# An attention and expert kernel on one core: the first token list's tables move to GpSimd, its planner keys are set anew, and eleven weight quarters instead of twelve go out ahead of it

## The chip, the core and the metric

The kernel runs on one core of a Trainium2 chip. Its engines are TensorE (PE, matmuls into PSUM), VectorE (DVE), ScalarE (ACT), GpSimd (POOL) and SyncE (SP). Each runs its own instructions in order, and they wait for each other through semaphores. Sixteen DMA engines serve the queues that SP, ACT and POOL issue to. POOL's own queue converts weights from fp32 to fp16 on the way.

The metric is device microseconds of one launch. Lower is better.

## The reference, cut to what matters

```python
def _attn_ref(q, k, v, is_retrieval, n_sink, window):     # 4 batches, 8 heads, 768 positions, 64 wide
    scores = scale * np.matmul(q, k.transpose(0, 1, 3, 2))
    stream_keep = causal & (is_sink | in_win)             # 4 sinks and a window of 64
    mask = np.where(retr, causal, stream_keep)            # heads 0, 2 and 6 see all that is causal
    a = np.exp(scores - max); a = a / (sum + 1e-09)
    return np.matmul(a, v)

def _moe_ref(x, w_skip, w_gate, w1, w2):                  # x: 3072 tokens x 512; 8 experts, 512 -> 1024 -> 512
    do_compute = x @ w_skip > 0
    out = x.copy(); xc = x[do_compute]
    logits = xc @ w_gate; e_idx = argmax(logits); gate_w = softmax(logits)[e_idx]
    for e in range(E):
        h = np.maximum(xc[e_idx == e] @ w1[e], 0.0)
        y[e_idx == e] = gate_w * (h @ w2[e])
    out[do_compute] = xc + y
```

The attention's output, its eight heads side by side, is x. About half of the tokens skip the experts, and each of the others goes to one expert.

## The kernel before

**Attention.** Two heads of a batch make a pair: 16 pairs, four to a batch, numbered 0 to 15. SP loads q and k of a pair and v of a whole batch. For pair i the steps are named as in the planner's calls:

- `Cq`, `Ck`, `Cv` (L712, L718): cast to fp16, nearly all on GpSimd. `Tq`, `Tk`, `Tv` (L740, L751): transposes on TensorE. `Oq` (ScalarE), `Ok` (VectorE, a few on ScalarE), `Ov` (VectorE): copies out of PSUM.
- `Vw`, `Ow`: the gate's columns v x w_gate are put beside v, so that the weighing gives the gate's logits too. `Kx`, `Vx` (L787, L823): GpSimd's copies for the heads with a window.
- `E`, `X`: scores in chunks of 1024 columns (TensorE, L886 and L898) and their exponential (ScalarE, L908).
- `PV` (L950): the weighing on TensorE, into one PSUM tile `opsa` that has a single buffer, so PV(i) waits for the normalisation of pair i-1.
- `Nr`, `Nl`, `Nx` (L969, L976, L986): reciprocal of the sums, gate logits, and x, on VectorE. Pair 15's Nx is on ScalarE (L1009), in 12 pieces. `Gs` (L1000): the logits of a batch summed over its heads.
- `xo` (L995): a batch's x is stored to the output. "Store 2" and "store 3" below are those of batches 2 and 3; store 3 is issued in two halves, one by SP and one by ACT.

**The two lists.** Tokens are sorted by expert into lists of 128 slots. The first list covers batches 0 to 2 (18 columns of 128 tokens), the second batch 3. `route` and `steps` (L1061, L1232) build them. The first list's chain is: the expert of each token (`mx` to `oh`, VectorE), its rank among the tokens of that expert (`ranks`, TensorE), the slot number in parts (`rsel` to `olo`, VectorE, some on GpSimd), and then two kinds of table: `L` (six of 3 columns, L1202) and `R` (three of 6 columns, L1192). The `slots` matmuls (L1226) multiply L by R; `fin_a` (L1438) turns the result into the indices `idx`.

**Experts.** A gather (L1310) fetches the 128 rows of a slot from the stored output, so the first one needs the indices and the stores of batches 0 to 2. Then come a cast (`cx`), a transpose (`tx`, L1368) and its copy (`ox`), the first matmuls (`F`, L1400), ReLU (ScalarE, L1411), the second matmuls (`Y`, L1422), the addition to the row (`A`, L1428), and a scatter back (L1320).

**Weights.** Each expert has w1 and w2, and each of these is loaded by two DMAs of 1 MB in HBM (512 KB as fp16 in SBUF, L445): a quarter of an expert. All go through GpSimd's queue. `PARTS` (L425) names, for each quarter issued during the attention, the step that it waits for; `late` (L1473) holds the others, issued between gathers and scatters in the order `GORDER`. The very last half matrix goes in two pieces of half that size.

**The order.** Two planners (class `Plan`, L55) write the program, one for the attention and one for the experts. Each step has an engine, an estimated duration, the steps that it needs, and a key. The planner simulates: when an engine is free, the ready step with the lowest key is next. The order in which steps start becomes the order of each engine's instructions. A pair's keys are ten times its number plus a constant of `K` (L647); the first list's steps on VectorE have keys from `K["r"]` up, its tables on GpSimd `K["rp"]`.

## Time and profile before

| | |
|---|---|
| time, median of 3 runs | 188.08 us (187.72 to 188.84) |
| the profiled execution | 187.94 us, of which its span is 186.2 us |
| mean granted TensorE clock | 0.927 |
| busy, share of the span | PE 80%, PEld 65%, DVE 59%, ACT 55%, POOL 70% |
| DMA | 47.12 MB in 27632 packets, mean 253 GB/s |
| HBM | 56.64 MB read, 10.49 MB written |

The profile page has the whole span in 40 slices of 4.65 us; a digit is the busy share in tenths. The attention fills the first half. From slice 21 the engines except GpSimd and the DMA engines have less to do for about four slices: this is where the lists are finished and the first tokens are gathered. After that the experts run to the end. A row of the table of stretches reads: the stretch, its length, the busy time of PE, PEld, DVE, ACT and POOL with the count of instructions, the granted TensorE clock, the mean busy share of the 16 DMA engines, and GB/s. A row of a timeline reads: start, time, engine, line, operation, tiles, shapes, count, and in brackets the idle time before it with what ended it.

### The profile page before, as it was taken

The numbers are of one execution on the slowest core, as the hardware profiler recorded it, in microseconds if no ns is written. First come the engines' busy times: TensorE is split into PE (matmuls) and PEld (weight loads), VectorE is DVE, ScalarE is ACT, GpSimd is POOL, SyncE is SP. The second block draws the span as 40 slices with busy tenths as digits, with TensorE's granted clock in tenths as the row PEclk, the third lists the DMA queues.
The fourth block names the chain that finished last, engine by engine and source line by source line (L and its number), as shares of the span: only waits on it lengthen the run. The fifth ranks groups of instructions, "written<-read, shape, count | busy, mean of one in ns | idle before, by whom it ended". The sixth has DMA issues, their size and how long they took to land.

```text
span 186.2 us, 4856 instructions
## 1 busy us (share of the span) xinstructions
PE 149.0 (80%) x1917; PEld 121.0 (65%) x1929; DVE 108.9 (59%) x245; ACT 103.3 (55%) x145; POOL 131.1 (70%) x229
## 2 busy tenths in 40 slices
PE   0697799699999989989825108999999999979900
PEld 0576688598888778878615108878769787838400
DVE  6565568677878758888994825045444266630320
ACT  2575889599898999999622981322224403403000
POOL 7566888989999999999790556484557788544440
PEclk9999999999999999999995555899999999999975
DMA  5999979998999899999999999999999999999520
GB/s 158 331 321 297 351 235 382 395 327 254 295 398 271 266 306 339 215 226 250 250 253 232 283 318 212 214 260 222 266 210 228 214 232 218 225 223 215 155 78 2
DMA packets 27632, 47.12 MB, mean 253 GB/s; under 512 B 5186, under 2 KB 19138, under 8 KB 27602
## 3 DMA queue, kind: packets, MB, share of 16 engines
q0 software_dynamic: 7312, 21.55, 53.9%
q1 hardware_dynamic: 18560, 23.99, 39.2%
q10 hardware_dynamic: 1730, 1.20, 2.0%
q8 instruction: 17, 0.28, 0.6%
q14 instruction: 13, 0.11, 0.2%
HBM read 56.64 MB, written 10.49 MB: 361 GB/s over the span
## 4 chain that ended last, share of the span: by engine, by line
DMA 41%; PE 23%; issue 11%; POOL 10%; ACT 5%; SPq 3%; DVE 3%; POOLq 0%; ACTq 0%
DMA w<-in_moe_w_dram 14%; DMA out_dram<-x 12%; PE pst L898 9%; DMA xg<-out_dram,idx 6%; PE opsa L950 5%; PE pst L886 4%; DMA out_dram<-xga,idx 4%; POOL out_dram L1320 4%; PE tps L740 4%; SPq L660 3%; DMA kf<-in_k_dram 3%; ACT at L908 3%; POOL w L445 2%; DMA qf<-in_q_dram 2%; POOL xg L1310 2%
## 5 line engine op out<-in xcount | busy, mean ns | idle before, releaser
L908 ACT ACTIVATE at<-pst 128x1024 f16<-128x1024 f32 (+1 forms) x60 | 58.8, 1013 | 9.3 <-PE pst L898 8.7
L1411 ACT ACTIVATE ht<-hps 128x512 f16<-128x512 f32 x32 | 17.1, 600 | 44.4 <-PE hps L1400 44.3
L898 PE MATMUL pst<-qT,k 128*128 128x128 f16 (+2 forms) x308 | 36.3, 238 | 0.7 <-ACT at L908 0.7
L1400 PEld LDWEIGHTS <-w 128*128 128x128 f16 x352 | 32.5, 148 | 3.8 <-DMA w<-in_moe_w_dram 1.5
L1400 PE MATMUL hps<-xT,w 128*128 128x128 f16 (+1 forms) x352 | 33.6, 258 | 1.6 <-DMA w<-in_moe_w_dram 1.0
L780 DVE COPY k<-tps 64x768 f16<-64x768 f16 x27 | 25.8, 954 | 13.1 <-PE tps L740 12.1
L898 PEld LDWEIGHTS <-k 128*128 128x128 f16 x308 | 24.8, 99 | 10.1 <-issue 3.3
L1422 PE MATMUL yps<-w,ht 128*128 128x512 f16 x128 | 30.5, 379 | 0.0
L950 PE MATMUL opsa<-va,at 128*128 128x74 f16 x392 | 21.0, 201 | 0.0
L445 POOL DMA_DIRECT2D w<-in_moe_w_dram x33 | 18.7, 574 | 2.1 <-DMA w<-in_moe_w_dram 1.7
L1422 PEld LDWEIGHTS <-ht 128*128 128x128 f16 x128 | 12.0, 98 | 11.7 <-issue 0.5
L950 PEld LDWEIGHTS <-at 128*128 128x128 f16 x472 | 19.2, 100 | 0.1
L1320 POOL DMA_INDIRECT out_dram<-xg,idx x10 | 10.4, 1037 | 11.8 <-DVE xg L1428 4.1
L886 PE MATMUL pst<-smask,identb 128*128 128x512 bf16 (+3 forms) x52 | 17.3, 345 | 1.6 <-ACT at L908 1.6
L1310 POOL DMA_INDIRECT xg<-out_dram,idx x10 | 11.8, 1179 | 7.8 <-DMA xga<-out_dram,idx 2.1
L986 DVE TENSOR_TENSOR x<-opsa,recs 128x768 f32<-128x768 f32 x15 | 14.1, 943 | 0.0
L1310 POOL DMA_INDIRECT xga<-out_dram,idx x6 | 6.5, 1078 | 10.8 <-DVE idx L1444 6.3
L1428 DVE SCALAR_TENSOR_TENSOR xg<-yps,gsl,xg 128x512 f32<-128x512 f32 x10 | 7.4, 746 | 11.2 <-PE yps L1422 11.0
L718 POOL CAST va<-vf 128x768 f16<-128x768 f32 x16 | 13.1, 823 | 1.1 <-DMA vf<-in_v_dram 0.5
L740 PE MATMUL tps<-ident,q 128*128 128x128 f16 x96 | 8.6, 230 | 6.5 <-DVE q L712 5.9
L712 POOL CAST k<-kf 128x768 f16<-128x768 f32 x15 | 12.4, 825 | 1.7 <-DMA kf<-in_k_dram 1.4
L766 ACT COPY qT<-tps 128x768 f16<-128x768 f16 x16 | 12.8, 800 | 1.0 <-PE tps L740 0.9
(147 smaller groups left out, 252.6 us busy)
## 6 DMA issues: line engine op xcount, KB each, us to landing
w<-in_moe_w_dram POOLq DMA_DIRECT2D x31, 512.0 KB
qf<-in_q_dram SPq DMA_DIRECT2D x16, 384.0 KB, 7.2
kf<-in_k_dram SPq DMA_DIRECT2D x15, 384.0 KB, 6.8
out_dram<-x SPq DMA_DIRECT2D x3, 1536.0 KB, 18.3
out_dram<-x SPq DMA_DIRECT2D x1, 768.0 KB
out_dram<-x ACTq DMA_DIRECT2D x1, 768.0 KB, 8.4
w<-in_moe_w_dram POOLq DMA_DIRECT2D x2, 256.0 KB
kf<-in_k_dram ACTq DMA_DIRECT2D x1, 384.0 KB, 4.4
```

Source lines behind the costliest of these rows:

```text
L445: nc.gpsimd.dma_start(out=wts[e, half][:, c], in_=(w1r, w2r)[half][e][:, c])
L740: nc.tensor.matmul(t[:, n], c16[w, i][:, n].rearrange("p h d -> p (h d)"), C.ident, is_transpose=True, start=(n == 0), stop=(n == NQB - 1))
L780: nc.vector.tensor_copy(to, ti)
L886: nc.tensor.matmul(pst[:, c0 - c * CH:c0 - c * CH + m].rearrange("p (n c) -> p n c", c=P), identb, mv, start=(n == 0), stop=(n == last))
L898: nc.tensor.matmul(pst[:, c0 - c * CH:c0 - c * CH + m * P], lt, qTs[i][:, qb * P:(qb + m) * P], start=(n == 0), stop=(n == last))
L908: nc.scalar.activation(ats[i][:, c * CH:c * CH + cn], psts[i, c][:, :cn], ACT.Exp, scale=SCALE)
L950: nc.tensor.matmul(opss[i][:, hi, qb * VA:(qb + 1) * VA], ats[i][:, b0 + c:b0 + c + P], vb, start=(n == 0), stop=(n == len(todo) - 1))
L1310: moved(nc.gpsimd.indirect_dma_start(out=row(t), out_offset=None, in_=out[:n, :], in_offset=bass.IndirectOffsetOnAxis(ap=idx[:, t:t + 1], ...
L1320: moved(nc.gpsimd.indirect_dma_start(out=out[:n, :], out_offset=bass.IndirectOffsetOnAxis(ap=idx[:, t:t + 1], axis=0), in_=row(t), in_offs ...
L1400: nc.tensor.matmul(hpss[n, b][:, fi, :], w1[:, s, m * b + fi], xTs[n][:, s, :w], start=(fi == 0 and s == 0), stop=(fi == m - 1 and s == DS ...
L1411: nc.scalar.activation(hts[n][:, m * b:m * (b + 1), :w], hpss[n, b], ACT.Relu)
L1422: nc.tensor.matmul(ypss[t], hts[n][:, j, c:c + P], w2[:, j], start=(j == 0), stop=(j == FS - 1))
```

## The change

Three things change in the code.

1. `PARTS` has 11 entries, not 12. Counted from zero, quarters 0 to 5 wait for the same steps as before, quarters 6 to 8 for Cv(15) instead of Vx(13), quarter 9 for Vx(14) instead of Vx(13), and quarter 10 for Vx(14) as before. The twelfth (the second part of expert 2's w2) goes to the late ones and becomes their first. Quarters 6 to 10 have their key lowered by 25.
2. All six L tables of the first list are made on GpSimd, where two (columns 12 to 17) were on VectorE. Two of the three R tables stay on VectorE, but their key is 900, behind every other step there. The planner's estimates for the R tables rise.
3. All constants of `K` are new but `sl`, `Wc` and `xa`.

```diff
-    PARTS = [("Cv", 8), ("Cv", 10)] + [("Vx", 10)] * 4 + [("Vx", 13)] * 4 + [("Vx", 14)] * 2
+    PARTS = [("Cv", 8), ("Cv", 10)] + [("Vx", 10)] * 4 + [("Cv", 15)] * 3 + [("Vx", 14)] * 2
...
-    TAB_DVE = dict(L=(12, 15), R=(6, 12))
+    TAB_DVE = (6, 12)
...
-        K = dict(r=152.5, rp=181, Cq=-144, Ck=-238, Cv=-205, W=-562.5, Tq=-7.5,
-                 Tk=-7.5, Oq=528.5, Ok=-84, OkA=-583, Kx=-828.5, Tv=-2.5,
-                 Ov=-4, Vw=-53, Ow=-472.5, Vx=-124, E=2.5, X=-65, PV=17,
-                 Nr=-46, Nl=114.1, Nx=-227.3, Gs=73.65, sl=-166.5, z=-127,
-                 Wc=-90, xa=-254, rk=-88)
+        K = dict(r=102.5, rp=333, Cq=-109.5, Ck=-161.5, Cv=-228.5, W=-850,
+                 Tq=-8, Tk=-5.5, Oq=421.5, Ok=-309.5, OkA=-680.5, Kx=-1173.5,
+                 Tv=-3.5, Ov=-33.5, Vw=-1, Ow=-941, Vx=-78, E=6, X=70.5,
+                 PV=16.5, Nr=-33.5, Nl=187.1, Nx=23.2, Gs=168.15, sl=-166.5,
+                 z=-19, Wc=-90, xa=-254, rk=-207)
...
-                10 * after[1] + K["W" if after[0] == "Vx" else "Wc"], rate=400)
+                10 * after[1] + K["W" if after[0] == "Vx" else "Wc"] - 25 * (n > 5), rate=400)
...
-                e = v if ph or m in TAB_DVE["R"] else nc.gpsimd
+                e = v if ph or m in TAB_DVE else nc.gpsimd
...
-                        e3 = v if m3 in TAB_DVE["L"] else nc.gpsimd
-                        fns["L", m3] = lambda m=m3, e=e3: e.tensor_tensor(
+                        fns["L", m3] = lambda m=m3: nc.gpsimd.tensor_tensor(
...
-                dve = ph or m in TAB_DVE["L"]
-                op(("r", ph, "L", m), "DVE" if dve else "POOL",
-                   0.9 if ph else 0.55 if dve else 0.8, f["L", m],
-                   [("r", ph, "rl" if ph else "ohi")], k0 + 0.3 if dve else K["rp"])
+                op(("r", ph, "L", m), "DVE" if ph else "POOL",
+                   0.9 if ph else 0.8, f["L", m],
+                   [("r", ph, "rl" if ph else "ohi")],
+                   k0 + 0.3 if ph else K["rp"])
...
-                dve = ph or m in TAB_DVE["R"]
+                dve = ph or m in TAB_DVE
                 op(("r", ph, "R", m), "DVE" if dve else "POOL",
-                   0.6 if ph else 0.55 if dve else 0.9, f["R", m],
+                   0.6 if ph else 0.85 if dve else 1.0, f["R", m],
                    [("r", ph, "oht"), ("r", ph, "glo")],
-                   k0 + 0.25 if dve else K["rp"])
+                   k0 + 0.25 if ph else 900 if dve else K["rp"])
```

## The prediction, made before the changed kernel had run

> **What bounds the kernel now.** I read the page first (clock, DMA and queue rows), then the table of stretches, the chain of waits backwards from the end, and the engines' timelines around the first list.
>
> ```profile
> span 186.2 us, 4856 instructions
> ...
> PEclk9999999999999999999995555899999999999975
> DMA  5999979998999899999999999999999999999520
> ...
> q0 software_dynamic: 7312, 21.55, 53.9%
> q1 hardware_dynamic: 18560, 23.99, 39.2%
> ```
>
> From slice 14 (65 us) to slice 37 the DMA row shows only nines, while TensorE's clock is halved for five slices: a stage that waits for data. The stretches say how full the 16 DMA engines are (second-last column; packets overlap a little, so "full" reads 1.05 to 1.07):
>
> ```profile
> 64.00:66.00 2.00, 2.00 (x39) 1.71 (x37) 1.54 (x2) 2.00 (x5) 1.88 (x4) 1.00 0.48 103
> ...
> 80.00:82.00 2.00, 2.00 (x48) 1.90 (x45) 1.84 (x4) 1.54 (x3) 1.96 (x5) 1.00 1.06 213
> 84.00:100.00 16.00, 11.77 (x197) 9.90 (x196) 13.46 (x29) 8.34 (x10) 11.82 (x21) 0.92 1.05 250
> ...
> 104.00:108.00 4.00, 0.35 (x6) 0.24 (x6) 2.47 (x12) 3.75 (x8) 3.34 (x4) 0.50 1.03 336
> 108.00:112.00 4.00, 0.61 (x4) 0.47 (x5) 1.31 (x7) 3.09 (x6) 1.67 (x3) 0.50 0.98 296
> 112.00:137.00 25.00, 24.55 (x258) 19.80 (x258) 9.88 (x19) 6.73 (x12) 15.44 (x18) 0.88 1.06 235
> 137.00:153.00 16.00, 16.00 (x133) 12.97 (x131) 8.25 (x18) 4.13 (x8) 11.47 (x12) 1.00 1.01 219
> ...
> 172.00:176.00 4.00, 4.00 (x19) 1.74 (x18) 1.50 (x2) 0.58 (x2) 1.96 (x2) 1.00 0.69 177
> ```
>
> After the hole at 64 to 66 us the DMA engines are full until about 173 us, except for 108:112 and 137:153. Every byte moved there has to be moved in any order. So whatever is done to the list, the last weight lands later or earlier only by the idle that is added or removed. The chain of waits ends in that stream:
>
> ```profile
> 78.96 22.64 DMA out_dram<-x
> ...
> 104.05 0.33 POOL xga L1310
> ...
> 157.50 14.58 DMA w<-in_moe_w_dram
> ```
>
> The weight issued at 157.50 lands at 172.1; two half-size pieces (256 KB written each) are queued behind it on GpSimd's ring. At the 213 GB/s of 80:82, where weights run almost alone, each takes 0.262 MB / 213 GB/s = 1.2 us (a quarter twice that, 2.5 us), so the last lands near 174.6. TensorE's timeline says how far its end is from that:
>
> ```profile
> 167.15 1.97 PE L1400 MATMUL hps<-xT,w 128*128 128x256 f16 x16 [1.05 <-DMA w<-in_moe_w_dram]
> ...
> 169.82 1.91 PE L1400 MATMUL hps<-xT,w 128*128 128x256 f16 x16
> 171.56 5.48 PE L1422 MATMUL yps<-w,ht 128*128 128x512 f16 x24
> ```
>
> It waits for a weight at 167.15 and ends at 177.04. Four matmuls (2 slots x 2) need the last piece, 4 x 5.48/24 = 0.9 us: with nothing else left over the end could be 174.6 + 0.9 = 175.5. **The bound is the DMA stream, and 1.5 us of TensorE's backlog stand behind it.**
>
> **The change, part by part.** The stage that it touches, from VectorE's, TensorE's, ScalarE's and GpSimd's timelines in this order:
>
> ```profile
> 93.23 1.65 DVE L1192 TENSOR_TENSOR tR<-r_oht,val 128x384 f16<-128x384 f16 x2
> ...
> 94.95 2.14 DVE L1202 TENSOR_TENSOR tL<-r_ohi,r_olo 128x384 f16<-128x384 f16 x2
> ...
> 97.19 0.94 DVE L986 TENSOR_TENSOR x<-opsa,recs 128x768 f32<-128x768 f32 x1
> ...
> 103.59 0.17 DVE L1444 SCALAR_TENSOR_TENSOR idx<-msb 128x8 int32<-128x8 f32 x1
> ...
> 110.59 0.62 DVE L1359 CAST x<-xga 128x512 f16<-128x512 f32 x1 [3.95 <-DMA xga<-out_dram,idx]
> ```
> ```profile
> 93.22 0.19 PE L950 MATMUL opsa<-vx,at 128*128 128x74 f16 x1
> ...
> 98.30 1.73 PE L950 MATMUL opsa<-va,at 128*128 128x74 f16 x25
> ...
> 100.21 0.26 PE L950 MATMUL opsa<-vx,at 128*128 128x74 f16 x1
> ```
> ```profile
> 101.20 2.56 ACT L1009 ACTIVATE x<-opsa,recs 128x64 f32<-128x64 f32 x12 [7.10 <-DVE lgh L976]
> ...
> 103.79 0.42 ACTq L995 DMA_DIRECT2D out_dram<-x  x1
> ```
> ```profile
> 93.45 4.32 POOL L1202 TENSOR_TENSOR tL<-r_ohi,r_olo 128x384 f16<-128x384 f16 x4 [0.31 <-DVE r_olo L1174]
> ```
>
> *Tables.* Pair 14's weighing (PV) ends at 93.4; its normalisation (Nx) ends only at 98.13, because the two R tables (1.65) and two L tables (2.14) stand ahead of it on VectorE. Pair 15 uses the same accumulator, so it starts at 98.30. The two L tables go to GpSimd, and the R tables get key 900, behind all normalisation. Nx(14) then needs 93.4 plus Nr, Nl, Nx, about 1.5 us: 95. That frees up to 3.1 us for pair 15, and it then runs before the clock halves (in the 96-to-100 us stretch), saving about 1 us of its 2.1. Store 3 (issued at 103.79) comes some 3.5 us sooner, at about 100. The R tables, 1.65 us, then end at about 97, before the L tables, and cost nothing; were they later than 100 they would hold slots.
>
> The price is on GpSimd: six L tables in place of four.
>
> ```profile
> L1202 POOL TENSOR_TENSOR tL<-r_ohi,r_olo 128x384 f16<-128x384 f16 x4 | 4.3, 1106 | 0.3 <-DVE r_olo L1174 0.3
> ...
> L1202 DVE TENSOR_TENSOR tL<-r_ohi,r_olo 128x384 f16<-128x384 f16 x2 | 2.1, 1107 | 0.0
> ```
>
> 6 x 1.106 = 6.6 from 93.45 ends at 100.1, the slots' matmuls at about 100.6; fin_a then writes the indices by 101.5 in place of 103.8, as they no longer wait behind pair 15 (its Nr, Nl, Gs and seven steps of the second list end by about 99). The first gather also needs store 2, landed at 78.96 + 22.64 = 101.60: I take an issue at 102 instead of 104.05, **2 us sooner**. Bounds: 3 us sooner if the chain starts earlier on VectorE (r's key falls from 152.5 to 102.5), nothing if slots stay ahead of pair 15 on TensorE and wait for 100.1.
>
> The Trainium skill's GPSIMD Engine Reference (section Engine selection) speaks against this: two-input elementwise work is about twice as slow on GpSimd as on VectorE. Here both engines take 1.11 us for the same table, so the trace disagrees; by the page, six tables of 2.2 would end at 106.7, and the gather would be late (last rival).
>
> *Weights.* One quarter fewer goes out before the list, so 2.5 us of transfer move behind the first gathers: nothing in the sum, as long as no hole opens in front of them. GpSimd's issues and casts now:
>
> ```profile
> 58.05 0.83 POOL L718 CAST va<-vf 128x768 f16<-128x768 f32 x1
> ...
> 68.30 2.70 POOL L445 DMA_DIRECT2D w<-in_moe_w_dram  x5
> ...
> 80.60 1.13 POOL L445 DMA_DIRECT2D w<-in_moe_w_dram  x2
> ...
> 83.94 0.82 POOL L718 CAST va<-vf 128x768 f16<-128x768 f32 x1
> ...
> 87.21 1.07 POOL L445 DMA_DIRECT2D w<-in_moe_w_dram  x2
> ```
>
> Before, six issues stand from 80.60 to 87.21; after, five come behind Cv(15) (83.94) and Vx(14), at 84 to 88. The ring is not empty then: five quarters issued at 68.30 to 71 take 5 x 2.5 us, stretched by the stores. So store 2 still shares with weights; I take its landing as unchanged (bounds: 4 us sooner if the ring runs dry, 1 later).
>
> The hole: before, store 3 and the first gather came when the ring ran dry (104:108 is 1.03). After, it runs dry 2.5 us sooner, and store 3 comes 3.5 us sooner, the gather 2 us. No new hole; 108:112 may fill: (1.06 - 0.98) x 4 = 0.3 us.
>
> *Keys moved along.* W's second quarter keeps key 10, but Cq(12) goes from -24 to 10.5 and Vx(9) from -34 to 12, so this issue now goes right behind Cv(10) (58.05) and not at 68.30. Its issue (2.70 / 5 = 0.54 us of GpSimd) then stands ahead of Cq(12) and Vx(9), and its transfer among the last q, k and v loads. By their keys no other issue of these six quarters passes a load. The rest of K reorders steps of equal length in a stage that ScalarE sets:
>
> ```profile
> L908 ACT ACTIVATE at<-pst 128x1024 f16<-128x1024 f32 (+1 forms) x60 | 58.8, 1013 | 9.3 <-PE pst L898 8.7
> ```
>
> Its cost lies between -3 us (a third of those 9.3 us idle) and +3 us; I take 0, as the longest of its waits falls under the same full DMA queue.
>
> **Sum**, against the profiled execution (187.94, span 186.2; 0.14 under the median of 188.08): 108:112, -0.3; half of the loss in 137:153, where (1.06 - 1.01) x 16 = 0.8, since scatters become ready earlier, -0.4; half of TensorE's 1.5 us backlog, because matmuls that now stand behind the wait at 167.15 have run before it when TensorE starts 2 us sooner, -0.8. Together -1.5: 186.4, or **186.6** on the scale of the median. Of the 2 us that the list gains, the stream hides the rest.
>
> **The rivals.**
> *Nothing comes through* (187.9, half of 108:112 at most). The list is early, but the stream ends when it did, and the in-order backlog behind 167.15 is the same. For it: the stretches at 1.06; the 0.8 us of 137:153 lie 30 us behind the list and may have another cause. Against: the first gather's data are waited for 3.95 us at 110.59. That the five quarters are not really "behind x" belongs here: they still share. The Trainium skill's DMA: Bandwidth & Descriptors (section Issuing engines are not separate DMA queues) says that transfers from all issuing engines interleave on the same 16 engines; store 2's 22.64 us for 1.5 MB, 69 of some 250 GB/s, agrees.
>
> *Slower: late loads of the last pairs empty the DMA later* (190.6). The place is the q and k loads of pairs 14 and 15:
>
> ```profile
> 65.14 0.42 SPq L660 DMA_DIRECT2D qf<-in_q_dram  x1
> ```
>
> They now run before the weights. If the earlier quarters overtake them, each load gets a share like store 2's (69 GB/s: 393 KB in 5.7 us), GpSimd's casts wait in order, and pairs 13 to 15 end late. From the point where store 3 is issued after about 101.5 (ring dry at 102 to 103, less a start of 1 to 2 us), the 2.5 us moved behind the list are an idle hole: 187.94 + 2.5 + 0.14 = 190.6.
>
> *More: the hole at 64:66 fills* with the quarter now issued near 59: (1.06 - 0.48) x 2 = 1.2 us more, 185.4.
>
> *GpSimd's tables at the page's rate*: slots at 107, the gather at 108, 4 us later than 104.05, into a stream that runs dry 2.5 us sooner: 188.08 + 6.5 = 194.6.
>
> **Chances.** Forecast 0.37; nothing 0.28; slower 0.23; more 0.09; tables slow 0.03. A measurement of this kernel tells about 0.5% (0.94 us) from no change. Faster by more: 0.33 of the forecast's 0.37 plus 0.09, 0.42; within: 0.04 and 0.28 and 0.02 of the slower case, 0.34; slower: 0.21 and 0.03, 0.24. The range holds forecast, nothing and both ends' prices: 184.9 (more, with half a us of the early gain) to 190.6; the slow tables lie outside. Cases of both signs hold much of it; the forecast's own range is 185.9 to 187.3.
>
> **What would show it.** Nx(14) ends near 95, pair 15's weighing starts before 97 at full clock, and store 3's ACT-queue issue is near 100: the tables step. Six L tables of about 1.1 us on GpSimd: the price. First gather at 102 and 108:112 at 1.05: the list. The last weight still lands at 173 to 175 while the first hidden matmul starts near 110.5: the bound. I am wrong if the share falls under 0.9 anywhere in 95 to 108, if store 2 lands before 98, if the casts of pair 15 wait for loads by more than 1 us, or if the last weight lands more than 1.5 us earlier.

## The result, and the profile after

| | before | after |
|---|---|---|
| time, median of 14 runs each | 188.1 us (185.49 to 190.47) | **190.41 us** (187.92 to 195.09) |
| the profiled execution | 187.94 us, span 186.2 | 188.45 us, span 186.8 |
| ratio after / before | | 1.0124, 95% interval 1.0077 to 1.0171 |

The change makes the kernel 1.2% slower. Two things matter for what follows. The times of the changed kernel spread over 7 us, and the profiled execution is one of its short ones, 2 us under its median: this one profile does not hold the loss. The ratios given here leave out runs over 1.5% above a kernel's fastest; as long runs are part of what is asked here, medians of all runs stand beside them.

The page of the changed kernel, with its clock and DMA rows and the two large queues:

```profile
span 186.8 us, 4867 instructions
...
PEclk9999997899999999999995559999999999999985
DMA  5999969998999989999999999999999999999520
...
q0 software_dynamic: 7312, 21.55, 54.1%
q1 hardware_dynamic: 18560, 23.99, 38.7%
```

The halved clock lasts three slices, where it was four and part of a fifth: the stage without work for TensorE became shorter. The bytes are the same. The table of stretches:

```profile
64.00:66.00 2.00, 2.00 (x28) 1.58 (x26) 1.24 (x3) 1.79 (x4) 1.95 (x3) 1.00 1.12 247
66.00:72.00 6.00, 5.34 (x99) 4.64 (x97) 3.50 (x7) 6.00 (x10) 5.71 (x13) 1.00 0.87 255
...
100.00:104.00 4.00, 0.76 (x11) 0.49 (x10) 3.62 (x22) 3.64 (x13) 1.81 (x3) 0.50 0.96 274
104.00:108.00 4.00, 0.34 (x6) 0.24 (x6) 0.91 (x3) 4.00 (x8) 3.63 (x5) 0.50 1.00 341
108.00:112.00 4.00, 2.75 (x25) 2.61 (x26) 2.81 (x9) 0.66 (x2) 1.98 (x2) 0.50 0.98 190
...
172.00:176.00 4.00, 2.85 (x18) 1.57 (x17) 0.00 (x0) 1.70 (x4) 2.05 (x3) 1.00 0.71 170
```

The hole at 64:66 is filled (1.12, was 0.48), but 66:72 has one (0.87, was 1.01), and 100:104 is a little emptier than before (0.96, was 1.07). TensorE has matmuls of the experts in 108:112 already (2.75 us busy, was 0.61). The timelines of GpSimd, VectorE, TensorE and ScalarE around the list:

```profile
95.03 5.40 POOL L1201 TENSOR_TENSOR tL<-r_ohi,r_olo 128x384 f16<-128x384 f16 x6 [0.31 <-DVE recs L969]
102.30 1.13 POOL L1309 DMA_INDIRECT xga<-out_dram,idx  x1 [1.88 <-DVE idx L1443]
```
```profile
95.26 0.94 DVE L986 TENSOR_TENSOR x<-opsa,recs 128x768 f32<-128x768 f32 x1
96.12 2.04 DVE L1192 TENSOR_TENSOR tR<-r_oht,val 128x384 f16<-128x384 f16 x2
```
```profile
96.25 0.99 PE L950 MATMUL opsa<-va,at 128*128 128x74 f16 x25
...
109.86 1.86 PE L1399 MATMUL hps<-xT,w 128*128 128x128 f16 x16 [0.58 <-DVE xT L1383]
...
168.37 1.97 PE L1399 MATMUL hps<-xT,w 128*128 128x256 f16 x16 [0.56 <-DMA w<-in_moe_w_dram]
170.88 1.97 PE L1399 MATMUL hps<-xT,w 128*128 128x256 f16 x16 [0.54 <-DMA w<-in_moe_w_dram]
174.00 3.61 PE L1421 MATMUL yps<-w,ht 128*128 128x512 f16 x16 [1.15 <-DMA w<-in_moe_w_dram]
```
```profile
101.36 0.42 ACTq L995 DMA_DIRECT2D out_dram<-x  x1
```

In this execution the list's stage does what the change is for: the first gather is issued 1.75 us sooner, the first hidden matmul follows at 109.86. At the end nothing of it is left: TensorE waits three times for a weight in the last 10 us of its work (before once, 1.05 us) and ends at 177.61 (before 177.04). Where the other 2 us of the median come from is seen only in longer executions of the same kernel.

### The profile page after: what moved, and what is told of

Read it like the earlier page. It is cut to its first block, busy times and chain, and to the rows that moved or that the text cites. A ratio compares the mean times of both kernels' runs of the same rounds, so it can differ in the third digit from the quotient of the medians.

```text
span 186.8 us, 4867 instructions
## 1 busy us (share of the span) xinstructions
PE 150.1 (80%) x1929; PEld 119.0 (64%) x1929; DVE 109.2 (58%) x243; ACT 103.2 (55%) x145; POOL 133.1 (71%) x231
## 4 chain that ended last, share of the span: by engine, by line
DMA 41%; PE 32%; issue 6%; SPq 5%; ACT 4%; POOL 4%; DVE 4%; POOLq 0%; DVEq 0%; ACTq 0%
DMA w<-in_moe_w_dram 12%; DMA out_dram<-x 11%; DMA qf<-in_q_dram 9%; PE pst L898 7%; PE hps L1399 7%; DMA xg<-out_dram,idx 5%; PE yps L1421 5%; PE pst L886 5%; SPq L660 4%; PE opsa L950 4%; POOL out_dram L1319 3%; DMA xga<-out_dram,idx 3%; PE tps L740 3%; ACT at L908 2%; PE tps L751 1%
## 5 line engine op out<-in xcount | busy, mean ns | idle before, releaser
L1410 ACT ACTIVATE ht<-hps 128x512 f16<-128x512 f32 x32 | 17.1, 600 | 48.0 <-PE hps L1399 47.9
L1399 PE MATMUL hps<-xT,w 128*128 128x128 f16 (+1 forms) x352 | 33.1, 252 | 2.1 <-DMA w<-in_moe_w_dram 1.5
L1399 PEld LDWEIGHTS <-w 128*128 128x128 f16 x352 | 31.3, 147 | 4.8 <-DMA w<-in_moe_w_dram 2.7
L886 PE MATMUL pst<-smask,identb 128*128 128x512 bf16 (+2 forms) x64 | 22.3, 359 | 2.1 <-ACT at L908 2.1
L950 PE MATMUL opsa<-va,at 128*128 128x74 f16 x392 | 20.3, 197 | 0.4 <-DVE x L986 0.3
L950 PEld LDWEIGHTS <-at 128*128 128x128 f16 x472 | 18.7, 98 | 0.8 <-DVE x L986 0.6
L1309 POOL DMA_INDIRECT xg<-out_dram,idx x10 | 11.2, 1115 | 8.6 <-ACT ht L1410 3.7
L712 POOL CAST q<-qf 128x768 f16<-128x768 f32 x14 | 11.5, 825 | 2.6 <-PE pst L898 1.7
L1358 DVE CAST x<-xg 128x512 f16<-128x512 f32 x10 | 6.0, 630 | 12.6 <-DMA xg<-out_dram,idx 12.5
## 6 DMA issues: line engine op xcount, KB each, us to landing
out_dram<-x SPq DMA_DIRECT2D x3, 1536.0 KB, 16.7
```

The costliest lines, as they stand in the source:

```text
L886: nc.tensor.matmul(pst[:, c0 - c * CH:c0 - c * CH + m].rearrange("p (n c) -> p n c", c=P), identb, mv, start=(n == 0), stop=(n == last))
L950: nc.tensor.matmul(opss[i][:, hi, qb * VA:(qb + 1) * VA], ats[i][:, b0 + c:b0 + c + P], vb, start=(n == 0), stop=(n == len(todo) - 1))
L1399: nc.tensor.matmul(hpss[n, b][:, fi, :], w1[:, s, m * b + fi], xTs[n][:, s, :w], start=(fi == 0 and s == 0), stop=(fi == m - 1 and s == DS ...
L1410: nc.scalar.activation(hts[n][:, m * b:m * (b + 1), :w], hpss[n, b], ACT.Relu)
```

## The experiments

Four theories were on the table in turn. **Q**: the weight quarter moved behind the list costs its transfer, as in the prediction's slower rival. **K**: the new keys put steps in a worse order. **S**: the new keys put Tv(4), the transposes of a v that is cast late, ahead of scores, and TensorE stands for 2 us near 27 us. **W**: the second weight quarter, issued 8 to 9 us sooner, makes store 1 (batch 1's x) late; batch 3's x uses the same buffer (there are two), so VectorE's Nx(12) waits for that store, and all that stands behind it on VectorE waits too: the list's chain, Nx(13), Nx(14).

Every run, with the kernel before run beside it on the same chip:

| run | made from | median us, range (runs) | before beside it | ratio [95%] |
|---|---|---|---|---|
| the change | | 190.41, 187.92–195.09 (14) | 188.1 | 1.0124 [1.0077, 1.0171] |
| e1_quarters | before | 191.87, 189.98–193.78 (6) | 187.49 | 1.0259 [1.0170, 1.0347] |
| e2_tables | before | 186.21, 184.52–188.88 (12) | 187.49 | 0.9965 [0.9926, 1.0004] |
| e3_keys | before | 195.12, 188.88–201.33 (6) | 187.49 | none |
| e4_no_quarters | after | 192.32, 188.12–195.91 (6) | 187.49 | none |
| e5_v4_later | after | 193.55, 190.37–197.37 (6) | 187.81 | 1.0159 [1.0083, 1.0235] |
| e6_before_v4_early | before | 186.95, 185.56–190.75 (6) | 187.81 | 0.9942 [0.9885, 0.9998] |
| e7_v4_later_12q | e5 | 194.13, 191.36–198.37 (6) | 187.81 | 1.0250 [1.0177, 1.0324] |
| e8_tab_quarters | after | 190.52, 189.69–194.05 (6) | 187.81 | 1.0146 [1.0093, 1.0199] |
| e9_w1_late | after | 187.02, 185.45–190.06 (12) | 187.12 | 0.9950 [0.9909, 0.9991] |
| e10_tab_w1_early | e2 | 187.75, 184.57–189.49 (12) | 187.12 | 0.9951 [0.9895, 1.0007] |
| e11_w1_v4_late | e9 | 188.64, 185.89–193.70 (13) | 187.12 | 1.0048 [0.9994, 1.0101] |
| e12_tab_11q | e2 | 188.37, 186.95–189.22 (12) | 187.12 | 1.0056 [1.0020, 1.0093] |
| f1_x3 | after | 187.76, 186.78–195.49 (12) | 186.81 | 1.0096 [1.0060, 1.0133] |
| f2_w1_late_12q | e9 | 187.38, 184.51–196.88 (12) | 186.81 | 0.9930 [0.9869, 0.9990] |
| f3_v4_later_x3 | e5 | 186.78, 185.05–198.00 (12) | 186.81 | 0.9979 [0.9940, 1.0017] |
| f4_after_again | after, unchanged | 189.38, 188.59–195.31 (7) | 186.81 | 1.0168 [1.0113, 1.0222] |
| g1_all | f2 | **186.40**, 183.99–193.52 (7) | 187.69 | **0.9874** [0.9807, 0.9940] |
| g2_tab_w1_early_x3 | e10 | 187.26, 185.74–189.62 (12) | 187.69 | 0.9982 [0.9944, 1.0020] |

### The parts of the change, one at a time (e1, e2, e3, e4, e8)

e1_quarters, the first part of the change alone:

```diff
-    PARTS = [("Cv", 8), ("Cv", 10)] + [("Vx", 10)] * 4 + [("Vx", 13)] * 4 + [("Vx", 14)] * 2
+    PARTS = [("Cv", 8), ("Cv", 10)] + [("Vx", 10)] * 4 + [("Cv", 15)] * 3 + [("Vx", 14)] * 2
...
-                10 * after[1] + K["W" if after[0] == "Vx" else "Wc"], rate=400)
+                10 * after[1] + K["W" if after[0] == "Vx" else "Wc"] - 25 * (n > 5), rate=400)
```

> The kernel before with one part of the change alone: eleven quarters in place of twelve, three of them behind Cv(15), two behind Vx(14), keys lowered by 25. Tables and K stay. Theory Q (the quarter that goes out behind the list is what costs; one quarter is 2.5 us of transfer): 1.2% slower than before, 190.4, and the last weight lands 1.5 to 2.5 us later than the 175.2 of before. Theory K (the new K costs, by the second quarter at 59 us and the loads behind it): no change, within 0.5% of before, last weight at 175.2 or earlier.

It came out 2.6% slower. VectorE's timeline of e1 tells why this is no test of the transfer:

```profile
92.15 1.65 DVE L1192 TENSOR_TENSOR tR<-r_oht,val 128x384 f16<-128x384 f16 x2
93.72 2.28 DVE L1202 TENSOR_TENSOR tL<-r_ohi,r_olo 128x384 f16<-128x384 f16 x2
95.92 0.34 DVE L976 TENSOR_TENSOR lgh<-opsa,recs 128x108 f32<-128x108 f32 x1
96.10 0.94 DVE L986 TENSOR_TENSOR x<-opsa,recs 128x768 f32<-128x768 f32 x1
```

With other due times the planner laid VectorE's whole chain and its four tables ahead of Nx(13), which starts at 96.1 where it started at 89.71 before. The first gather went out at 106.0. The planner re-orders on any small edit, so an edit through the planner tests an order, not the thing edited.

e2_tables, the second part alone (tables on GpSimd, R on VectorE with key 900, all else of before):

```diff
-    TAB_DVE = dict(L=(12, 15), R=(6, 12))
+    TAB_DVE = (6, 12)
...
-                   k0 + 0.25 if dve else K["rp"])
+                   k0 + 0.25 if ph else 900 if dve else K["rp"])
```

> The kernel before with the tables' part alone: six L tables on GpSimd, two R tables at key 900; K, the twelve quarters and their keys stay. Both theories: within 0.5% of before, 187.5 to 188.5. Nx(14) ends before 96 in place of 98.1 and the first gather is issued at 102 to 103.5 in place of 104.05, with the last weight unchanged at about 175. If it is slower by over 0.5%, the tables themselves cost, and both theories lack a term.

0.9965, by the medians 186.21 beside 187.49: the tables step alone is a small gain at most, as the interval reaches 1.0004. Its first gather stands at 102.05.

e3_keys, the new `K` alone:

```diff
-        K = dict(r=152.5, rp=181, Cq=-144, Ck=-238, Cv=-205, W=-562.5, Tq=-7.5,
+        K = dict(r=102.5, rp=333, Cq=-109.5, Ck=-161.5, Cv=-228.5, W=-850,
...
```

> The kernel before with the new K alone: the second quarter goes out near 59.7 in place of 68.3; tables stay divided as before, twelve quarters wait for the same steps as before. Theory K: 1 to 1.5% slower, 190 to 191, with a stretch after 64 us in which the DMA share falls, as 0.87 in 66 to 72 after the change. Theory Q: within 0.5% of before.

The slowest of all by its median, but again for an order of its own: the tables are still VectorE's there, and r = 102.5 puts them ahead of pair 13's normalisation (Nx(13) at 98.3, gather at 108.1).

e4_no_quarters, the change with the twelve quarters of before:

```diff
-    PARTS = [("Cv", 8), ("Cv", 10)] + [("Vx", 10)] * 4 + [("Cv", 15)] * 3 + [("Vx", 14)] * 2
+    PARTS = [("Cv", 8), ("Cv", 10)] + [("Vx", 10)] * 4 + [("Vx", 13)] * 4 + [("Vx", 14)] * 2
...
-                10 * after[1] + K["W" if after[0] == "Vx" else "Wc"] - 25 * (n > 5), rate=400)
+                10 * after[1] + K["W" if after[0] == "Vx" else "Wc"], rate=400)
```

> The changed kernel with the quarters as they were: twelve, four behind Vx(13), two behind Vx(14), no lowered keys; tables and K as changed. Theory Q: 187 to 188.3, that is 1 to 2% under the changed kernel and not slower than before. Theory K: 190 to 191, as the changed kernel.

Giving the quarter back gained nothing (192.32), which speaks against Q, though weakly: Nx(13) starts at 95.7 by the planner's order.

e8_tab_quarters, the change with the old `K`:

```diff
-        K = dict(r=102.5, rp=333, Cq=-109.5, Ck=-161.5, Cv=-228.5, W=-850,
+        K = dict(r=152.5, rp=181, Cq=-144, Ck=-238, Cv=-205, W=-562.5, Tq=-7.5,
...
```

> The changed kernel with all constants of K as before: tables on GpSimd and eleven quarters, no stall at 27.4. Theory S: the first gather at 101.5 to 102.5, ahead of the end of the ring at 104.4; within 0.6% of the tables alone, 185.5 to 187.5. Theory Q: 1 to 2% over the tables alone, 188 to 190.

1.0146, with Nx(13) at 96.8 by order. So the old keys give the other two parts no better order, and none of the three parts can be priced by leaving it out through the planner. From here on an edit either keeps every engine's order of compute steps or is read by its profile.

### The stall near 27 us (e5, e6, e7)

TensorE's and ScalarE's timelines of the changed kernel have a stall that before had not:

```profile
29.43 0.51 PE L751 MATMUL tps<-ident,va 128*128 128x128 f16 x6 [2.04 <-POOL va L718]
```
```profile
31.32 1.02 ACT L908 ACTIVATE at<-pst 128x1024 f16<-128x1024 f32 x1 [2.65 <-PE pst L898]
```

Exponential 15, counted from zero, starts 2.4 us later (35.3, before 32.9). e5_v4_later moves Tv(4) back behind E(3,2), and keeps Tq(5) behind E(3,3):

```diff
-            op(("Tq", i), "PE", 0.33, transpose(i, "q"), [("Cq", i), "ident"],
+            op(("Tq", i), "PE", 0.33, transpose(i, "q"), [("Cq", i), "ident"] + [("E", 3, 3)] * (i == 5),
-            op(("Tv", i), "PE", 0.33, transpose_v(i), [("Cv", i), "ident"],
+            op(("Tv", i), "PE", 0.33, transpose_v(i), [("Cv", i), "ident"] + [("E", 3, 2)] * (i == 4),
```

> The changed kernel with one step moved back: Tv(4), the transposes of pair 4's v, stands on TensorE behind E(3,2) again, as in the kernel before, and not right behind E(3,1), where it waits 2.04 us for its cast at 27.4 to 29.4 us. Theory S (this stall makes the whole attention 1.5 to 2 us late, and the shorter ring of weights has no slack for it): the 16th exponential starts at 32 to 33 us in place of 35.3, the last one ends at 93 to 94 in place of 95.7, the time is 186 to 188, 1.5 to 2.2% under the changed kernel. Theory Q (the stall is hidden under the full DMA queue; the quarter that goes out behind the list costs): 189.5 to 190.5, as the changed kernel.

193.55, slower still, against what S said. But the edit only shortened the stall: in its profile TensorE still stands 1.44 us for that cast. Nor does the order alone make it: e9 and f1 below have TensorE's order of the change, and their profiles have the stall at 0.23 and 0.41 us, because the cast ends sooner there. What speaks plainly against S is the profile of f2, also below. It has the whole stall, and its execution is 186.83 us long, 1.6 us under that of the change; TensorE's timeline:

```profile
30.16 0.51 PE L751 MATMUL tps<-ident,va 128*128 128x128 f16 x6 [2.01 <-POOL va L718]
```

So S falls as the main cause, and what the stall costs stays unpriced. e5's profile showed W. The chain of waits of e5, then its timelines of VectorE and ScalarE:

```profile
69.16 19.90 DMA out_dram<-x
```
```profile
89.08 0.96 DVE L986 TENSOR_TENSOR x<-opsa,recs 128x768 f32<-128x768 f32 x1 [4.14 <-DMA out_dram<-x]
```
```profile
93.11 1.02 ACT L908 ACTIVATE at<-pst 128x1024 f16<-128x1024 f32 x1 [5.37 <-PE pst L898]
```

Store 1 is issued at 69.16 and lands at 89.06. VectorE wants to write batch 3's x into its buffer at 84.94 and stands 4.14 us. The copies and sums that TensorE needs stand behind it on VectorE, and at 93.11 ScalarE has been idle for 5.37 us.

e6_before_v4_early puts the early Tv(4) into the kernel before:

```diff
+                *([("Tv", 4)] if (i, c) == (3, 2) else [])], 10 * i + K["E"] + c / 10)
...
+                      ("Tv", 4) if i == 2 else None],
```

> The kernel before with this one step alone moved: Tv(4) stands ahead of E(3,2) and PV(2,0), as in the changed kernel; all keys, tables and quarters stay. Theory S: TensorE waits about 2 us near 27.5, the 16th exponential starts near 35, the last ends near 96, the first gather goes out at 105.5 to 106.5 in place of 104.05, and the time is 1 to 2% over before, 189.5 to 191. Theory Q: within 0.5% of before.

0.9942: no loss, but there the cast was not late and no stall appeared, so it says nothing of S's price.

e7_v4_later_12q is e5 with the twelve quarters of before:

```diff
-    PARTS = [("Cv", 8), ("Cv", 10)] + [("Vx", 10)] * 4 + [("Cv", 15)] * 3 + [("Vx", 14)] * 2
+    PARTS = [("Cv", 8), ("Cv", 10)] + [("Vx", 10)] * 4 + [("Vx", 13)] * 4 + [("Vx", 14)] * 2
...
-                10 * after[1] + K["W" if after[0] == "Vx" else "Wc"] - 25 * (n > 5), rate=400)
+                10 * after[1] + K["W" if after[0] == "Vx" else "Wc"], rate=400)
```

> The changed kernel with Tv(4) moved back and twelve quarters as before. Theory S: as the kernel with the tables alone, 185.5 to 187.5, and within 0.5% of the same with eleven quarters, since the list is there before either ring is dry. Theory Q: 1% or more under the changed kernel with eleven quarters and Tv(4) moved back.

1.0250. The same wait is in its timeline of VectorE, and the table of stretches has the hole that follows:

```profile
88.30 0.96 DVE L986 TENSOR_TENSOR x<-opsa,recs 128x768 f32<-128x768 f32 x1 [2.08 <-DMA out_dram<-x]
```
```profile
104.00:108.00 4.00, 0.84 (x15) 0.60 (x12) 3.15 (x16) 2.70 (x13) 0.00 (x0) 0.50 0.20 41
```

The weights issued ahead of the list have all landed, the first gather goes out only at 108.06, and for four microseconds the DMA engines do a fifth of what they can.

### The store's wait itself (e9, f4, f1, f3, e11)

e9_w1_late is the change with one DMA issue moved: the second quarter's, from 59.73 back to 67.90. The order of all other instructions is that of the change.

```diff
-                place(h) if h >= NPRE and a == 0 else load_part(h, a, a + 4),
+                [load_part(0, 0, 4), lambda: None,
+                 lambda: (load_part(0, 4, 8)(), load_part(1, 0, 4)())][n]
+                if n < 3 else load_part(h, a, a + 4),
```

> The changed kernel with one DMA issue moved: the second weight quarter goes out right ahead of the third, near 69 us, as in the kernel before, and not behind Cv(10) near 59.7; every other instruction of every engine stays in its place. Theory W (the early quarter shares the DMA engines with the last v load and pushes the store of batch 1 into the weights behind it; Nx(12) on VectorE writes that store's buffer and waits, and all pairs behind it are late): store 1 lands at 79 to 82 in place of 85.1 to 89.1, no wait of Nx(12) for it, and the time is 186 to 188, 1 to 2% under the changed kernel, with little spread. Rival K (other parts of the new order cost, such as the wait at 27.4): 189.5 to 191, as the changed kernel.

187.02 and 0.9950, where the change has 190.41 and 1.0124: by the ratios **that one issue is the loss**, 1.7%. f4_after_again ran the changed kernel unchanged, to catch a long execution in a profile.

> The changed kernel once more, for a second profile and runs beside the others of this call: 189.5 to 191.5, with a spread of over 5 us between its runs. Theory W: a run over 190 shows Nx(12) waiting for store 1 by 1 us or more and a share under 0.8 between 100 and 108 us; a run at 188 shows neither.

It caught one (span 192.8). The view of the DMAs issued in 62 to 69 us gives store 1's time from issue to landing, for before, the change and e9 in turn (the row of f4 is from a window to 77, its store 1 is issued at 70.69):

```profile
out_dram<-x SPq DMA_DIRECT2D x1, 1536.0 KB, 14.0
```
```profile
out_dram<-x SPq DMA_DIRECT2D x1, 1536.0 KB, 16.7
```
```profile
out_dram<-x SPq DMA_DIRECT2D x1, 1536.0 KB, 8.0
```
```profile
out_dram<-x SPq DMA_DIRECT2D x1, 1536.0 KB, 19.8
```

SP's timeline adds when it is issued, for before and the change:

```profile
65.65 0.42 SPq L995 DMA_DIRECT2D out_dram<-x  x1
```
```profile
68.42 0.42 SPq L995 DMA_DIRECT2D out_dram<-x  x1
```

Then f4's timeline of VectorE, the view of L995 with who waited for it, its table of stretches and GpSimd's timeline:

```profile
90.54 0.96 DVE L986 TENSOR_TENSOR x<-opsa,recs 128x768 f32<-128x768 f32 x1 [4.00 <-DMA out_dram<-x]
```
```profile
who waited for it (us, times):
  DVE x L986: 4.0, 1
```
```profile
104.00:108.00 4.00, 1.87 (x43) 1.40 (x40) 3.83 (x8) 1.76 (x9) 3.89 (x5) 0.93 0.17 33
```
```profile
109.78 1.14 POOL L1309 DMA_INDIRECT xga<-out_dram,idx  x1 [1.88 <-DVE idx L1443]
```

Beside the short profile of the same kernel: the gather is 7.5 us later, the hole is 0.83 x 4 = 3.3 us, the span 6.0 us longer. 1.4 us of that are there when Nx(12) is wanted (86.54 against 85.10), the rest is the wait and what it sets off. Put together by profile, with Nx(12) "wanted" at its start less its wait:

| run | span | store 1 landed | Nx(12) wanted | wait | first gather |
|---|---|---|---|---|---|
| before | 186.2 | 79.7 | 86.5 | 0 | 104.05 |
| e2 | 182.8 | 79.3 | 85.8 | 0 | 102.05 |
| the change, short | 186.8 | 85.1 | 85.1 | 0 | 102.30 |
| the change, long (f4) | 192.8 | 90.5 | 86.5 | 4.00 | 109.78 |
| e5 | 191.6 | 89.1 | 84.9 | 4.14 | 108.55 |
| e7 | 190.1 | 88.3 | 86.2 | 2.08 | 108.06 |
| e9 | 186.2 | 73.8 | 84.6 | 0 | 101.9 |
| f2 (below, quarter late) | 185.1 | 83.7 | 84.1 | 0 | 103.25 |
| e11 (below, quarter late) | 191.9 | 88.0 | 84.5 | 3.51 | 106.78 |
| f1 (three buffers) | 185.3 | 87.2 | 83.6 | 0 | 101.24 |
| f3 (three buffers) | 184.3 | 87.4 | 84.4 | 0 | 102.14 |
| g1 (three buffers, quarter late) | 191.8 | 95.1 | 84.7 | 0 | 112.38 |

In its profile before has 7 us to spare and the change none, so that each execution of the change wins or loses a race; its times spread from 188 to 195. f1_x3 takes away only the reason to wait, a third buffer for x; all instructions stand in the order of the change:

```diff
-                    xsb[b] = x_pool.tile([P, NQB, DM], FP32, tag="x", bufs=2,
+                    xsb[b] = x_pool.tile([P, NQB, DM], FP32, tag="x", bufs=3,
```

> The changed kernel with three x buffers in place of two, and every instruction of every engine where it was: batch 3 no longer writes the buffer that store 1 reads, so Nx(12) needs nothing of store 1; the second quarter still goes out near 59.7 and still shares with the last loads. Theory W (the cost is Nx(12)'s wait for store 1): 186.5 to 188, as with the quarter moved. Rival B (the early quarter costs by the shares of the DMA engines alone, whoever waits): 189.5 to 191, as the changed kernel.

Its store 1 is as late as ever (87.2), and Nx(12) no longer cares. The timelines of VectorE and GpSimd in f1:

```profile
83.64 0.95 DVE L986 TENSOR_TENSOR x<-opsa,recs 128x768 f32<-128x768 f32 x1
```
```profile
101.24 1.14 POOL L1309 DMA_INDIRECT xga<-out_dram,idx  x1 [2.30 <-DVE idx L1443]
```

The median falls from 189.38 (f4, measured beside it) to 187.76; the ratio only from 1.0168 to 1.0096. So Nx(12)'s wait is 0.7 of the 1.7% by the ratio, more than half of the loss by the medians, and 1% stays. f3_v4_later_x3 is e5 with the same third buffer, that is, with Tv(4) moved back as well:

```diff
-                    xsb[b] = x_pool.tile([P, NQB, DM], FP32, tag="x", bufs=2,
+                    xsb[b] = x_pool.tile([P, NQB, DM], FP32, tag="x", bufs=3,
```

> The kernel with Tv(4) moved back, where Nx(12) waited 4.14 us for store 1, with three x buffers. Theory W: 186 to 188 in place of 193.5, no idle before Nx(12), the first gather before 103. Rival B: 191 to 194.

From 193.55 to 186.78, from 1.0159 to 0.9979, by one number in the code: the strongest single evidence for W. Why f1 keeps 1% (1.0096) where f3 keeps nothing stays open. The stall does not tell: it is 0.41 us in f1's profile and 1.08 in f3's.

The third buffer does not end the long runs either: f1 has one of 195.49, f3 has 193.71 and 198.00. Of the 124 runs of before none is over 190.90. Over 192 us are 6 of the change's 21 (f4's with them), 3 of 37 with the quarter late and two buffers (e9, e11, f2) and 4 of 31 with three buffers (f1, f3, g1). So the wait for store 1 is one reason of long runs, and under the new keys there is at least one more.

e11_w1_v4_late has e9's late quarter and e5's later Tv(4), with two buffers:

```diff
+            op(("Tq", i), "PE", 0.33, transpose(i, "q"), [("Cq", i), "ident"] + [("E", 3, 3)] * (i == 5),
+            op(("Tv", i), "PE", 0.33, transpose_v(i), [("Cv", i), "ident"] + [("E", 3, 2)] * (i == 4),
```

> The changed kernel with both moves: the second quarter near 69 us, and Tv(4) behind E(3,2). Theory W: store 1 is no longer waited for, so the 1.5 to 2 us that Tv(4) cost may now come through: 185 to 187, at or up to 1% under the same with the quarter alone moved. Rival K: if the quarter is not the cause, 191 to 194, as with Tv(4) alone moved.

The sum of two gains was not there: 1.0048, 188.64. Its profile is of its longest run (193.7) and has the wait again, 3.51 us, with store 1 landing at 88.0 although the second quarter is late. So the late issue does not exclude the wait. With the quarter late alike, store 1 lands at 83.7 in f2 and 95.1 in g1, and only e9's profile has it at 73.8. One thing tells these apart. Four or five weight quarters go out together, starting between 66.9 and 72.1 us in every profile, and e9's store 1 is issued 2.1 us ahead of them, by its timelines of SP and GpSimd:

```profile
65.80 1.33 SPq L995 DMA_DIRECT2D out_dram<-x  x1
```
```profile
67.90 2.70 POOL L445 DMA_DIRECT2D w<-in_moe_w_dram  x5
```

In f2, e11 and g1 it is within 0.4 us of them. Over all profiles: in the nine where store 1 has a lead under 0.5 us, or none (the change, f4, e5, e7, e11, f1, f2, f3, g1), it takes 16.3 to 26.9 us, in the eleven others, with leads of 0.8 to 4.7 us, 8.0 to 17.1. So the early quarter, behind which SP issues store 1 later, goes with a lost lead (2.65 us before, 0.44 in the change). No run sets the lead by itself; this is read from the traces and not shown.

### The early quarter and the quarter behind the list (e10, g2, e12, f2), and a version with all (g1)

e10_tab_w1_early puts the early second quarter into e2, with all orders kept:

```diff
-            op(("Cv", i), "POOL", 0.85, cast_v(i),
+            op(("Cv", i), "POOL", 0.85, cast_v(i) if i != 10 else
+               lambda: (cast_v(10)(), load_part(0, 4, 8)()),
...
+                load_part(h, a, a + 4) if n != 1 else lambda: None,
```

> The kernel with the tables alone (median 186.2) and the same issue moved the other way: the second quarter goes out behind Cv(10) near 58.5; everything else stays in its place. Theory W: store 1 lands after 84 in place of 79.3, Nx(12) waits for it, and the time is 1 to 3% over the tables alone, 188.5 to 191.5. Rival K: within 0.6% of the tables alone, or up to 1 us faster, as the stretch of 60 to 66 us fills.

W expected a loss and the ratio shows none (0.9951, e2 0.9965); by the medians of all runs, each beside its own before, there is one of 1% (1.0034, e2 0.9932). The profile, of one of the shorter runs, says how that one escaped: store 1 landed at 84.8 (79.3 in e2), and Nx(12) wanted the buffer at 85.6. So store 1 lands 5.5 us later there as well, and the margin, 6.5 us in e2, still held in the profiled run. g2_tab_w1_early_x3 adds the third buffer to e10 (`bufs=3` as in f1):

> The tables alone with the second quarter early and three x buffers: the early quarter fills the DMA engines near 64 us and can no longer hold Nx(12). Theory W: no slower than the tables alone (0.9965 of before), 185 to 186.5. If the early quarter's shares cost by themselves: 187.5 or more.

0.9982, by the medians 0.9977, between e2 and e10: too near to both to tell whether e10's longer runs had the wait.

e12_tab_11q moves the twelfth quarter of e2 behind the list, orders kept:

```diff
-                place(h) if h >= NPRE and a == 0 else load_part(h, a, a + 4),
+                load_part(h, a, a + 4) if n != 11 else lambda: None,
...
+        late = [part(5, 4, 8)] + late
```

> The kernel with the tables alone and eleven quarters ahead of the list, with the order of all steps of the attention kept: the twelfth quarter's issue is left out there and is the first of the late ones. Theory W (a quarter moved behind the list costs nothing of itself; the 2.6% of the quarters' part alone came from the order that the planner then laid): within 0.6% of the tables alone, 185.5 to 187.3. Theory Q (it is the later quarter): 1 to 2.5% over the tables alone, 188 to 190.5.

1.0056 against 0.9965: here the quarter behind the list costs 0.9%, and TensorE's timeline of e12 shows two of its waits for weights at the end, where e2 has one of 0.20:

```profile
170.59 1.97 PE L1399 MATMUL hps<-xT,w 128*128 128x256 f16 x16 [0.48 <-DMA w<-in_moe_w_dram]
173.78 3.61 PE L1421 MATMUL yps<-w,ht 128*128 128x512 f16 x16 [1.22 <-DMA w<-in_moe_w_dram]
```

f2_w1_late_12q gives e9 the twelfth quarter back ahead of the list:

```diff
-                if n < 3 else load_part(h, a, a + 4),
+                if n < 3 else load_part(h, a, a + 4) if n < 10
+                else lambda: (load_part(5, 0, 4)(), load_part(5, 4, 8)()),
...
```

> The changed kernel with the second quarter near 68 us and the twelfth quarter issued early again, right behind the eleventh; nothing else moved in the attention. If the quarter that moved behind the list costs 0.9% of itself, as the two kernels with the tables alone say: 185 to 186.3, 1 to 1.5% under the kernel before and 0.5 to 1% under the same with eleven. If it costs nothing once the list is early: 186.5 to 187.5, the same as with eleven.

0.9930 against 0.9950: no difference (by the medians of all runs 1.0031 and 0.9995, with two long runs, 195.03 and 196.88). Why the same quarter costs 0.9% under the old keys and nothing under the new ones stays open.

g1_all has all four edits: the late second quarter, twelve quarters, the later Tv(4), three buffers.

```diff
+                 lambda: (load_part(0, 4, 8)(), load_part(1, 0, 4)())][n]
...
+            op(("Tv", i), "PE", 0.33, transpose_v(i), [("Cv", i), "ident"] + [("E", 3, 2)] * (i == 4),
...
+                    xsb[b] = x_pool.tile([P, NQB, DM], FP32, tag="x", bufs=3,
```

> The changed kernel with all four edits: the second quarter near 68 us, the twelfth quarter early, Tv(4) behind E(3,2), three x buffers. Theory W: with no wait for store 1 left in any execution and 1.5 to 2 us less at 27.4, 184.5 to 186, 1 to 1.5% under the kernel before. If the DMA stream alone sets the end by now: 186.5 to 187.5, as with the single edits.

**0.9874 [0.9807, 0.9940]**: faster than both kernels, with five of its seven runs between 183.99 and 186.62. Its median of all, 186.40, is 0.7% under before's and a little over what W said. Its profile is of the longest run (193.52), and a buffer does not help there. The chain of waits and GpSimd's timeline:

```profile
79.93 31.45 DMA out_dram<-x
```
```profile
112.38 1.14 POOL L1312 DMA_INDIRECT xga<-out_dram,idx  x1 [11.92 <-DMA out_dram<-x]
```

Store 2 takes 31.45 us there, and the first gather, which reads it, waits 11.92 us. In this run store 1 landed only at 95.1. Store 2 follows it on SP's queue and landed 14.0 us behind it in f4, 17.8 in e11 and 16.3 here (111.4). So a late store 1 may well reach the gather through store 2 too, with a third buffer or without; no run tried to cure it.

## Why the prediction was wrong, step by step

**Tables: right, in the main.** Nx(14) ends at 96.2 (said: near 95; in the kernel before 98.13), pair 15's weighing starts at 96.25 at full clock (said: before 97), store 3's issue by ACT is at 101.36 (near 100), the first gather at 102.30 (102), the first hidden matmul at 109.86 (110.5). e2 has the step alone, worth 0.35% by the ratio, if anything. The row of L1201 with least, median and greatest nanoseconds shows that the price per table was taken too high:

```profile
L1201 POOL TENSOR_TENSOR tL<-r_ohi,r_olo x6: 824/829/1143, 95.0 to 99.6; 128x384 f16<-128x384 f16 x6
```

Six tables took 5.40 us, not 6.6: the 1106 of before was measured beside VectorE's tables.

**Weights behind the list ("nothing in the sum"): open.** e12 against e2 says 0.9%, f2 against e9 says nothing. The bound itself held: the last weight lands at 176.4 (said: 173 to 175), and TensorE waits for weights up to the end.

**108:112 (-0.3), 137:153 (-0.4) and half of the backlog (-0.8): wrong in sign or empty.** 108:112 stayed at 0.98 and 137:153 at 1.01, and the 1.5 us of backlog became waits: 0.56, 0.54 and 1.15 us in the last 10 us. TensorE was early at 110 and idle at 168; of the list's gain the stream hid all, as the rival *nothing comes through* had it. In e2 some of it may have come through.

**"Keys moved along … I take 0": the step that failed.** Its first half was right: the second quarter does go out behind Cv(10), at 59.73 (said: near 59), among the last loads. The cost of that was looked for only on those loads. The queue that it passes also holds store 1, on SP behind these loads: issued at 68.42 where it was at 65.65, and then 16.7 to 19.8 us on its way where it was 14.0. What the term comes to is the difference between the change (1.0124) and e9 (0.9950): 1.7%, some 3.3 us, where 0 stood with a bound of +3. With it taken out, the rest of the change is at 0.9950 of before, on the side of the forecast (186.6 / 188.08 = 0.9921). And the trace of before had the margin in it, unread. Store 1 landed at 65.65 + 14.0 = 79.7, and its buffer was next written at 86.54, by this row of VectorE's timeline:

```profile
86.54 0.94 DVE L986 TENSOR_TENSOR x<-opsa,recs 128x768 f32<-128x768 f32 x1
```

Of these 6.9 us the change takes 5.4 (landing at 85.1) to 10.8 (90.5). One sign that the prediction named for being wrong, a share under 0.9 between 95 and 108 us, is missing in the short profile (0.96, 1.00) and there in the long one (0.17).

**The rival *late loads of the last pairs empty the DMA later*** (0.23) had the right place (the early second quarter), the right end (a hole in the DMA in front of the first gather: 3.3 us in f4) and nearly the right time (190.6; the median is 190.41), but the wrong victim, so that its time is right by luck. In the two profiles of the change the casts behind 70 us wait for no load, or for 0.59 us (f4); waits of 1.01 (e5), 1.99 (f1) and 3.04 (e7) do occur in kernels made from it. **The hole at 64:66 fills** came true (1.12), and came back at 66:72 (0.87): nothing was won.

**What stays open.** By the ratios the early quarter is the loss, and Nx(12)'s wait for store 1 is the part of it that a buffer takes away: 0.7 of 1.7% from the change to f1, all of it from e5 to f3. How the rest of it reaches the end is not shown: f1 (1.0096) stands over e9 (0.9950), though by the medians beside their own before the difference is 0.6%. e10 against e2, under the old keys, shows nothing by the ratio and 1% by the medians. No run sets store 1's lead over the weights by itself, and none tells what makes the long runs that stay with three buffers, but for the one in g1's profile.

## What to carry to other kernels

When a DMA is issued earlier, list everything behind it on every queue that it now shares the engines with, and for each store ask which buffer it still holds and who writes that buffer next: the margin is the landing against the first write, and it can be read from the trace before the change is made. A kernel whose times spread by 4% may have a race in it, as this one has, and a single profile may show the side on which it is won: profile it again until a long execution is caught. If a planner orders the code, test a suspicion by an edit that keeps all orders (one issue moved, one buffer more), because every key or due time that is changed tests another program.

## What the runs showed of the hardware

**The same store of 1.5 MB took 8.0 to 31.5 us.** It was 8.0 us in e9, where it went out 2.1 us ahead of the weights, 14.0 before, 16.7 and 19.8 in two executions of one program, and 31.5 (store 2, g1). At 8.0 us it moves 196 GB/s, at 19.8 us 79. How much the weight queue moves in the 20 us from 57 to 77 does not order these times: its share is 23.5% in e9 and 38.3% in f4, but 19.8% in e11, where store 1 takes 20.7 us. The Trainium skill's DMA: Bandwidth & Descriptors (section Queues, rings and completion order) says that each engine takes one packet from each queue with work in turn. The times agree with that as far as a store is slow when weights are issued together with it and quicker when it is issued first; no run here shows the turns themselves.

**A table on GpSimd costs more than one on VectorE, and each slows the other.** Before's row for the R tables of VectorE (the least is that of the smaller list):

```profile
L1192 DVE TENSOR_TENSOR tR<-r_oht,val x3: 350/546/1180, 93.2 to 105.4; 128x384 f16<-128x384 f16 x2, 128x192 f16<-128x192 f16 x1
```

The first such table takes 546 ns, with GpSimd's first L table beginning 0.2 us after it, and the second 1180 beside the L tables. An L table, as large, takes 829 on GpSimd with no table on VectorE and 1143 beside VectorE's. By these, 829 / 546 = 1.5, though of two different tables. The third R table, made on GpSimd while VectorE had other steps, took 1145 there, 2.1 times 546. The prediction compared 1106 with 1107 and called the engines equal, but both numbers were of two engines in each other's way. The Trainium skill's GPSIMD Engine Reference (section Engine selection), which has GpSimd about twice as slow, is nearer to the runs than that comparison was.
